# Planning the issue order of a recurrent attention kernel from a table of TensorE places, with a hand-over latency for each pair of engines

## The chip, the cores and the metric

The kernel runs on one core of one Trainium2 chip. The metric is the device time of one execution in microseconds (us), as the median over several executions. "The profile" is one execution recorded by the hardware profiler; its page and its trace give each instruction's engine, start, duration and what it waited for. In the profile PE is TensorE (PEld are its weight loads), DVE is VectorE, ACT is ScalarE, POOL is GpSimd, SP is SyncE. "L968" is a line of the kernel file; the same operation has another line number in each variant.

## The reference

Two rounds of attention with a recurrent memory and of a dense layer. All the tensors are bf16.

```python
def attention(x, mem0, Wq, Wk, Wv, Wo):        # x: 2048 x 512, 32 heads of 128
    mem = mem0                                  # 8 rows of 512
    for s in range(64):                         # 64 segments of 32 rows
        h = concat([mem, xs])                   # 40 rows
        q, k, v = h @ Wq, h @ Wk, h @ Wv
        p = softmax(mask(q k^T * scale))        # memory columns open, the rest causal
        o = (p @ v) @ Wo
        mem = o[:8]                             # read by the next segment
        outs.append(o[8:])
    return concat(outs)

x = x + attention(layernorm(x), ...);  x = x + relu(layernorm(x) @ w1) @ w2   # 512 -> 1376 -> 512
x = x + attention(layernorm(x), ...);  x = x + relu(layernorm(x) @ w1) @ w2
```

The segments of one attention are a chain: the queries of a segment need the last output projection of the segment before.

## The kernel before

Both attentions run interleaved, the second one four segments behind the first, in 68 steps. One step projects queries and keys for 5 units of heads (u0 to u4), makes scores and a softmax for each, transposes the probabilities P into PT, attends, and ends with the output projection, whose memory rows VectorE copies into HT for the next queries. Work of the values, the layernorms and the dense layers is put between.

The program is not written in issue order. Each operation is recorded in a `Plan` with its cost, what it reads and what it writes; a list scheduler in Python then chooses, when the kernel is built, the order, the buffers, and for some operations one of two engines. The framework adds the semaphores afterwards, from the memory that each instruction really touches. Two things about that matter in this case: it takes the instructions in the order in which the plan emits them, and it keeps accesses of two engines to one PSUM bank apart, even where both only read. The plan knows nothing of the second.

```python
LAT = (0.26, 0.16, 0.16, 0.20, 1.70)            # hand-over latency, one for each engine
def t_act(n): return 0.09 + 0.833e-3 * n
def t_dve(n, rate=1): return 0.085 + 1.042e-3 * n / rate
...
# order(): 3 passes, each forward (list scheduling) and backward (latest start = next priority),
# corrected by AHEAD[kind]; the best of the three is kept and emitted in order of planned start
```

One PSUM bank (`wo`, tile "st" in the profile) holds the result of the output projection, and two copies read it: VectorE takes the memory rows into HT, and ScalarE or VectorE takes the output rows into OX.

```python
plan.op(DVE, 0.15, ev, r=[wo], w=[("HTm", i)])                        # the HT copy
...
copy_op(NC4 * SEG * len(aa), rows, r=[wo, "zero ox"], w=[ox])          # the OX copy, on ACT or DVE
```

PT is copied out of PSUM in two halves, partitions 0 to 63 and 64 to 127, and each half goes to the engine that the plan finds free first.

```python
for b in range(2):
    def keep(eng, b=b):
        R = slice(64 * b, 64 * b + 64)
        copy_on(eng, PT[R, a_lo:a_hi, 0:2 * nx, b, :], tp[R, A]...)     # cut
    copy_op(n, keep, r=[tp, "zero PT"], w=[PT, (PT, b)] if b == 0 else [(PT, b)])
```

Eight loads bring the attention's weights. The plan gives each a fixed time of arrival by its place in this list.

```python
for i, part in enumerate(("v0", "v2", "q0", "k0", "q2", "k2", "o0", "o2")):
    ...
    plan.op(POOL, 1.0, dma, w=[("W", c, pc), ("W", c, pc + 1), ...], lag=0.0)
    for n in range(2):
        plan.available(("W", c, pc + n), 4.0 + LOAD * (i + 1) + ...)
```

Of the kernel before, what the change touches and what calls it, by code (L numbers as in the profile page):

```python
# [20 lines left out]



PE, ACT, DVE, POOL, SP = range(5)
LAT = (0.26, 0.16, 0.16, 0.20, 1.70)

WHOLE, COL64, EITHER = range(3)
TURN = 0.11
PASSES = 3

RULE = (0.052, 0.937, 39.167, 24.322)
AHEAD = {
    "attend.ev": -1.96, "attend.mm": -0.95, "dense_layer.mm": -0.85, "dense_layer.relu": 5.2, "finish_pair.add": -5.1,
    "finish_pair.add0": 0.5, "finish_pair.add1": -6.36, "finish_pair.turn": 2.26, "finish_pair.widen": 0.01,
    "late_values.cp": -9.2, "late_values.put": 0.92, "layernorm.aggr": -7.15, "layernorm.keep": 0.04,
    "layernorm.norm": -2.92, "layernorm.power": -0.26, "layernorm.stats": 2.48, "layernorm.turn": -30.25,
    "load_dense.dma1": -1.13, "load_dense.dma2": -2.4, "load_group.get": -0.77, "load_weights.dma": -0.55,
    "make_ident": 4.63, "make_mask": 7, "place_values.dma": 17.27, "prep_x.cp": -1.81, "prepare.get_memory": -2.96,
    "prepare.get_x": -8.86, "prepare.keep": -0.84, "prepare.place": 0.28, "prepare.zero": -0.64,
    "prepare.zero_banks": -5.82, "prepare.zero_columns": -5.11, "prepare_group.load": -0.14,  # L40
    "prepare_group.put": -0.18, "project.ev": 10.38, "project.first": 0.18, "project.mm": -0.98,
    "project.rows": -4.33, "queries_keys.ev": 4.81, "queries_keys.mm": 0.09, "scores.block": 0.96,
    "scores.exp": -1.91, "scores.keep": -25.3, "scores.mm": 0.21, "scores.mul": -8.63, "scores.recip": -1.72,
    "scores.sub": -9.57, "scores.top": 1.48, "scores.total": 48.55, "scores.turn": 1.1, "values.mm*": -36.32,
# [6 lines left out]

def t_act(n):
    return 0.09 + 0.833e-3 * n


def t_dve(n, rate=1):
    return 0.085 + 1.042e-3 * n / rate


def t_pool(n):  # L60
    return 0.06 + 2.2e-3 * n


class Pool:
# [5 lines left out]
    def reset(self):  # L70
        self.free, self.taken = [(0.0, i, None) for i in range(len(self.tiles))], 0
# [7 lines left out]
    def when(self, bufs):  # L79
        if len(self.free) < len(bufs) or self.ordered and bufs[0].no != self.taken:  # L80
            return 1e9
        return sorted(f[:2] for f in self.free)[len(bufs) - 1][0]

    def take(self, b):
        f = min(self.free, key=lambda f: f[:2])
        self.free.remove(f)
        self.taken += 1
        b.i = f[1]
        return f[2]
# [12 lines left out]
class Op:  # L102
    __slots__ = ("eng", "cost", "fn", "preds", "succs", "bufs", "new", "given", "ready", "start", "end", "wait",
                 "after", "seq", "tile", "lag", "mode", "more", "both", "spare")


class Plan:
    def __init__(self):
        self.ops, self.writer, self.readers = [], {}, {}
        self.given = {}  # L110
# [4 lines left out]
    def op(self, eng, cost, fn, r=(), w=(), tile=WHOLE, lag=None, more=0.0, spare=False):  # L115
        o = Op()
        o.both = dict(zip(eng, cost)) if isinstance(eng, tuple) else None
        if o.both:
            eng, cost = eng[0], cost[0]
        o.eng, o.cost, o.fn, o.succs, o.seq, o.tile = eng, cost, fn, [], len(self.ops), tile  # L120
        o.mode, o.more, o.spare = tile, more, spare
        o.lag = LAT[eng] if lag is None else lag
# [26 lines left out]
    def forward(self, prio):  # L149






        look, stay, far, room = RULE
        for pool in self.pools:
            pool.reset()
        for b in self.bufs:
            b.left, b.end = len(b.users), 0.0  # L160
        for o in self.ops:
            o.wait, o.ready, o.after = len(o.preds), o.given, []
        free = [0.0] * 5
        cand = [[] for _ in range(5)]
        for o in self.ops:
            if not o.wait:
                for e in o.both or (o.eng,):
                    cand[e].append(o)
        count, tile = 0, WHOLE
        while count < len(self.ops):  # L170
            best = None
            for e in range(5):
                lo, starts = None, []
                for o in cand[e]:
                    t = max(o.ready, free[e])
                    if o.both and any(max(o.ready, free[i]) + c < t + o.both[e] for i, c in o.both.items() if i != e):
                        continue
                    for pool, bufs in o.new:
                        t = max(t, pool.when(bufs))
                    starts.append((t, o))  # L180
                    if lo is None or t < lo:
                        lo = t
                if lo is not None and lo < 1e9 and (best is None or lo < best[0]):
                    best = (lo, e, starts)
            assert best is not None, "no operation can be planned"
            lo, e, starts = best
            def rank(c):
                return (prio[c[1].seq] - (stay if e == PE and c[1].tile in (tile, EITHER) else 0.0), c[1].seq)

            t, o = min((c for c in starts if c[0] <= lo + look), key=rank)  # L190
            if e == PE and o.spare:

                soon = [c for c in starts if t < c[0] < t + o.cost and prio[c[1].seq] < prio[o.seq] - far]
                if soon:
                    due = min(c[0] for c in soon)
                    t, o = min((c for c in starts if c[0] + room * c[1].cost * c[1].spare <= due and c[0] <= due), key=rank)
            o.start = t
            for i in o.both or ():
                if i != e:
                    cand[i].remove(o)  # L200
            if o.both:
                o.eng, o.cost, o.lag = e, o.both[e], LAT[e]
            cand[e].remove(o)
            for pool, bufs in o.new:
                for b in bufs:
                    last = pool.take(b)
                    if last is not None:
                        o.after += last.users
            o.end = o.start + o.cost
            if e == PE:  # L210
                o.mode = tile if o.tile == EITHER else o.tile
                if o.mode != tile:
                    o.end, tile = o.end + TURN, o.tile
                if o.mode == COL64:
                    o.end += o.more
            free[e] = o.end
            seen = o.end + o.lag
            for b in o.bufs:
                b.left -= 1
                b.end = max(b.end, seen)  # L220
                if not b.left:
                    b.pool.free.append((b.end, b.i, b))
            for s in o.succs:
                s.ready = max(s.ready, seen)
                s.wait -= 1
                if not s.wait:
                    for i in s.both or (s.eng,):
                        cand[i].append(s)
            count += 1
        return max(o.end for o in self.ops)  # L230

    def backward(self, total):

        due = [total] * len(self.ops)
        users = [list(o.preds) + o.after for o in self.ops]
        wait = [len(o.succs) for o in self.ops]
        for o in self.ops:
            for p in o.after:
                wait[p.seq] += 1
        free = [total] * 5  # L240
        heaps = [[] for _ in range(5)]
        later = [[] for _ in range(5)]

        def offer(o):
            heappush(later[o.eng], (-due[o.seq], o.seq))

        for o in self.ops:
            if not wait[o.seq]:
                offer(o)
        late, count, tile = [0.0] * len(self.ops), 0, WHOLE  # L250
        while count < len(self.ops):
            best = None
            for e in range(5):
                hi = free[e] if heaps[e] else -1e9
                if later[e]:
                    hi = max(hi, min(free[e], -later[e][0][0]))
                if best is None or hi > best[0]:
                    best = (hi, e)
            hi, e = best
            while later[e] and -later[e][0][0] >= hi - 0.05:  # L260
                o = self.ops[heappop(later[e])[1]]
                heappush(heaps[e], (-o.end, o.seq))
# [822 lines left out]
```

## Time and profile before

The median is 1677.74 us (3 runs, 1676.78 to 1678.85). The table shows where TensorE's time goes. It is worked out from the starts of all matmuls in the trace: the floor is the count of each form times its usual start-to-start spacing, and what is above it is sorted by where it occurs. (The parts overlap a little: as rounded they exceed the span by 2 us here.)

| part of the profiled 1679.0 us | us |
|---|---|
| floor: matmuls at their usual spacing | 1535 |
| 495 changes between 128- and 64-column mode, median 0.097 each | 48 |
| waits between operations | 71 |
| stalls inside operations | 27 |

These are the busy times and the shares of the chain that ended last, from the page of the kernel before.

```profile
PE 1628.4 (97%) x40568; PEld 1395.6 (83%) x40568; DVE 1066.3 (64%) x3090; ACT 1061.1 (63%) x2679; POOL 246.3 (15%) x603
...
PE 79%; DVE 13%; DMA 4%; issue 1%; POOL 1%; ACT 1%; SPq 0%; POOLq 0%; DVEq 0%; ACTq 0%
```

TensorE bounds the kernel. The next fence has lines of the view of waits of the same kernel, four of TensorE's, without those between them: engine and line, what it was idle for, total us, how often, the longest.

```profile
PEld L832 <- DVE HT L990: 9.4, 21, 0.5
PE work L832 <- DVE HT L990: 6.7, 21, 0.3
PE work L947 <- ACT PT L724: 6.1, 24, 0.3
PEld L519 <- DVE P L909: 5.4, 26, 0.9
```

The first two are the queries behind the HT copy, then attend behind PT, then the transposition of P behind the softmax. No single wait is large. By the matmul starts, waits and stalls together come to 1.84 us per two steps in steady state (steps 26 to 61).

The last view of before is that of the HT copy: its instructions, what ended the idle time of its engine, and who waited for it.

```profile
L990 DVE CAST HT<-st x67: 191/225/227, 60.3 to 1647.5; 128x64 bf16<-128x64 f32 x60, 128x32 bf16<-128x32 f32 x7
its engine sat idle before it (us, times) until:
  PE st L974: 81.3, 65
  ACT OX L724: 0.5, 1
who waited for it (us, times):
  ACT OX L724: 44.9, 65
```

The HT copy waits for TensorE, as it should, and the OX copy on ScalarE waits for the HT copy, because both read one bank and the HT copy was emitted first.

### The profile page before, as it was taken

To read this page: it belongs to the slowest core of one execution; us is meant where nothing else is said; L and a number is where in the kernel's file an instruction comes from. 1 tells how busy PE (TensorE), PEld (TensorE's weight loads), DVE (VectorE), ACT (ScalarE), POOL (GpSimd) and SP (SyncE) were. 2 spreads that over 40 slices of the span, in tenths; PEclk is the share of its full clock that TensorE was granted. 3 is DMA by queue.
4 is the path that set the end of the run, shared out by engine and by line. 5 is a ranking of instruction groups with operands and counts; after the bars stand their busy time and mean duration, and the time that the engine had idled before them with its cause. 6 is when DMAs were issued, how large, how long until landed. Compare 5 with 4: busy or idle time off the path is not lost.

```text
span 1679.0 us, 90465 instructions
## 1 busy us (share of the span) xinstructions
PE 1628.4 (97%) x40568; PEld 1395.6 (83%) x40568; DVE 1066.3 (64%) x3090; ACT 1061.1 (63%) x2679; POOL 246.3 (15%) x603
## 2 busy tenths in 40 slices
PE   6899999999999999999999999999999999999998
PEld 3578888888888888888888888888888888888886
DVE  5457576666676575667666666676566666766665
ACT  3466666666666666666666666666666666666664
POOL 3111111111111111111111111111111111111100
PEclk9999999999999999999999999999999999999999
DMA  9611111111110101000000000101010000000000
GB/s 366 239 51 35 37 39 27 35 39 34 33 39 18 37 18 31 22 21 24 19 24 21 22 20 17 27 18 26 17 27 16 21 22 21 18 20 17 18 5 7
DMA packets 32502, 64.88 MB, mean 39 GB/s; under 512 B 7048, under 2 KB 16912, under 8 KB 32112
## 3 DMA queue, kind: packets, MB, share of 16 engines
q1 hardware_dynamic: 25984, 39.38, 8.5%
q0 software_dynamic: 4608, 18.19, 2.9%
q8 instruction: 318, 5.21, 1.3%
q10 hardware_dynamic: 1520, 1.52, 0.3%
q14 instruction: 72, 0.59, 0.1%
HBM read 33.89 MB, written 12.45 MB: 28 GB/s over the span
## 4 chain that ended last, share of the span: by engine, by line
PE 79%; DVE 13%; DMA 4%; issue 1%; POOL 1%; ACT 1%; SPq 0%; POOLq 0%; DVEq 0%; ACTq 0%
PE work L832 33%; PE fill L780 16%; PE st L974 13%; PE fill L519 8%; PE work L947 3%; PE work L861 3%; DMA Wo_sb<-in_A_Wo_dram 3%; PE work L519 2%; DVE sm L886 2%; DVE OT L726 2%; DVE PT L726 2%; DVE ln L528 1%; DMA V<-vw 1%; POOL P L909 1%; DVE xg L616 1%
## 5 line engine op out<-in xcount | busy, mean ns | idle before, releaser
L832 PE MATMUL work<-HT,Wq_sb 128*128 128x80 bf16 (+1 forms) x8704 | 391.0, 200 | 8.7 <-DVE HT L990 6.7
L832 PE MATMUL work<-HT,Wk_sb 128*128 128x80 bf16 (+1 forms) x8704 | 389.7, 199 | 5.3 <-DMA Wk_sb<-in_A_Wk_dram 2.8
L974 PE MATMUL st<-OT,Wo_sb 128*128 128x80 bf16 (+1 forms) x8704 | 353.6, 200 | 3.7 <-DMA Wo_sb<-in_A_Wo_dram 3.5
L832 PEld LDWEIGHTS <-Wq_sb 128*128 128x128 bf16 x8704 | 333.0, 99 | 28.3 <-issue 9.9
L974 PEld LDWEIGHTS <-Wo_sb 128*128 128x128 bf16 x8704 | 321.7, 100 | 24.2 <-issue 17.8
L832 PEld LDWEIGHTS <-Wk_sb 128*128 128x128 bf16 x8704 | 335.9, 99 | 7.0 <-DMA Wk_sb<-in_A_Wk_dram 3.7
L872 DVE TENSOR_TENSOR es<-work,maskb 128x320 f32<-128x320 f32 (+2 forms) x340 | 137.3, 404 | 303.6 <-PE work L861 295.3
L909 POOL TENSOR_TENSOR P<-es,sm 128x160 bf16<-128x160 f32 (+1 forms) x274 | 127.5, 466 | 1212.2 <-ACT kT L724 494.2
L780 PE MATMUL fill<-Wv_sb,HT 128*64 128x512 bf16 x2176 | 282.7, 384 | 0.6 <-DVE vg L726 0.6
L724 ACT CAST qT<-work 128x320 bf16<-128x320 f32 (+1 forms) x500 | 204.6, 409 | 83.7 <-PE work L832 63.3
L724 ACT CAST kT<-work 128x320 bf16<-128x320 f32 (+1 forms) x489 | 200.0, 409 | 74.4 <-PE work L832 29.4
L724 ACT CAST PT<-work 64x320 bf16<-64x320 f32 (+2 forms) x451 | 162.7, 363 | 111.8 <-PE work L519 69.1
L724 ACT CAST vw<-fill 128x512 bf16<-128x512 f32 x221 | 129.3, 585 | 103.1 <-PE fill L780 94.6
L724 ACT CAST OT<-work 128x320 bf16<-128x320 f32 (+1 forms) x374 | 145.1, 409 | 58.7 <-PE work L947 56.9
L780 PEld LDWEIGHTS <-HT 128*64 128x64 bf16 x2176 | 102.3, 110 | 63.7 <-issue 3.2
L883 ACT ACTIVATE es<-es 128x320 f32<-128x320 f32 (+2 forms) x340 | 135.1, 404 | 23.4 <-DVE es L879 13.9
L886 DVE TENSOR_REDUCE sm<-es 128x8 f32<-128x320 f32 (+2 forms) x340 | 133.4, 399 | 25.3 <-ACT es L883 22.7
L876 DVE TENSOR_REDUCE mx<-es 128x8 f32<-128x320 f32 (+2 forms) x340 | 135.0, 397 | 3.2
L879 DVE TENSOR_TENSOR es<-es,mx 128x320 f32<-128x320 f32 (+2 forms) x340 | 134.2, 401 | 1.6
L861 PEld LDWEIGHTS <-qT 128*40 128x40 bf16 x4096 | 91.5, 98 | 43.3
L726 DVE CAST PT<-work 64x160 bf16<-64x160 f32 (+2 forms) x229 | 87.3, 381 | 60.3 <-ACT PT L724 47.0
L947 PE MATMUL work<-PT,V 128*64 128x80 bf16 (+1 forms) x1504 | 114.8, 203 | 7.5 <-ACT PT L724 5.9
(89 smaller groups left out, 1856.2 us busy)
## 6 DMA issues: line engine op xcount, KB each, us to landing
V<-vw SPq DMA_DIRECT2D x252, 48.0 KB
V<-vh SPq DMA_DIRECT2D x126, 64.0 KB
vh<-vg SPq DMA_DIRECT2D x12, 512.0 KB
Wv_sb<-in_A_Wv_dram POOLq DMA_DIRECT2D x2, 2048.0 KB, 11.1
Wq_sb<-in_A_Wq_dram POOLq DMA_DIRECT2D x2, 2048.0 KB, 22.3
Wk_sb<-in_A_Wk_dram POOLq DMA_DIRECT2D x2, 2048.0 KB, 29.2
Wo_sb<-in_A_Wo_dram POOLq DMA_DIRECT2D x2, 2048.0 KB, 42.5
vh<-w_sb SPq DMA_DIRECT2D x4, 512.0 KB
```

The costliest lines, as they stand in the source:

```text
L519: nc.tensor.matmul(out_[u:v, :], lhsT=lhsT[:, u:v], rhs=rhs, start=start, stop=stop, tile_position=(0, u))
L724: nc.scalar.copy(out=out_, in_=in_)
L726: nc.vector.tensor_copy(out=out_, in_=in_)
L780: nc.tensor.matmul(vp[64 * b:64 * b + 64, :], lhsT=cols[:, c4, :], rhs=Wv_sb[:, c4, n * 512:(n + 1) * 512], start=(c4 == 0), stop=(c4 == N ...
L832: nc.tensor.matmul(qp[:, hi * 2 * L:hi * 2 * L + n], lhsT=W_sb[:, c4, h * Dh:(h + 1) * Dh], rhs=HT[:, c4, c0:c1], start=(c4 == 0), stop=(c ...
L861: nc.tensor.matmul(v[64 * g2:64 * g2 + L, a, b, i, :], lhsT=qT[:, hi, a * L:(a + 1) * L], rhs=kT[:, hi, a * L:(a + 1) * L], start=True, st ...
L872: nc.vector.tensor_tensor(out=flat(es[:, A]), in0=flat(sp[:, A]), op=ALU.add, in1=maskb[:, a_lo:a_hi, :].unsqueeze(2).to_broadcast([128, n ...
L883: nc.scalar.activation(out=es[:, A], in_=es[:, A], func=ACTF.Exp, scale=SCALE)
L886: nc.vector.tensor_reduce(out=sm[:, As], in_=es3(), axis=AX.X, op=ALU.add)
L909: (nc.gpsimd if eng == POOL else nc.vector).tensor_tensor(out=o, in0=e, in1=sv.unsqueeze(3).to_broadcast([128, na, 2, L]), op=ALU.mult)
L947: nc.tensor.matmul(o[u:u + cols, :, a, :], lhsT=V[:, p, e0 + u:e0 + u + cols], rhs=PT[:, a, 2 * i + h2, :, :], start=True, stop=True, tile ...
L974: nc.tensor.matmul(wo[:, 2 * W * c4 + c0:2 * W * c4 + c1], lhsT=Wo_sb[:, h, c4 * 128:(c4 + 1) * 128], rhs=OT[:, h, c0:c1], start=(h == 0 a ...
```

## The change

The change replaces the planner and its model, and nothing of what is computed: both kernels record the same 9896 operations with the same dependencies. The three passes become one. TensorE's operations get their priority from a table, by their place in a period of two steps; the operations of the other engines get theirs from their successors. The latencies become a table with one entry for each pair of engines, and the costs are made smaller. The table looks as if it was searched for by trial.

```diff
-LAT = (0.26, 0.16, 0.16, 0.20, 1.70)
+LAT = ((0.0, 0.20, 0.21, 0.26, 0.26), (0.155, 0.14, 0.14, 0.20, 0.20), (0.145, 0.18, 0.125, 0.23, 0.23),
+       (0.13, 0.13, 0.10, 0.10, 0.20), (1.7, 1.7, 1.7, 1.7, 1.7))     # rows: from, columns: to; PE ACT DVE POOL SP
-TURN = 0.11
-PASSES = 3
+TURN = 0.096
+PERIOD = 17.9985
+PLACE = {
+    ("attend.mmu0.0", 0): 181.486, ("attend.mmu0.0", 1): 97.524, ...    # cut: one number per operation and step parity
+}
 def t_act(n):
-    return 0.09 + 0.833e-3 * n
+    return 0.05 + 0.833e-3 * n
 def t_dve(n, rate=1):
-    return 0.085 + 1.042e-3 * n / rate
+    return 0.065 + 1.042e-3 * n / rate
+    def rank_ops(self):
+        for o in reversed(self.ops):
+            if PE in o.cost:
+                o.prio = PERIOD * o.step + PLACE.get((o.key, o.step % 2), 0.0)
+            else:
+                e, c = min(o.cost.items(), key=lambda x: x[1])
+                o.prio = min((s.prio - (LAT[e][min(s.cost)] if o.lag is None else o.lag) for s in o.succs),
+                             default=PERIOD * (o.step + 3)) - c - AHEAD.get(o.kind, 0.0)
-    def forward(self, prio): ...      # cut
-    def backward(self, total): ...    # cut
```

A few costs of single operations change by some hundredths, those of GpSimd's copies by more (0.06 + 0.0013 n in place of 0.06 + 0.0022 n for n columns), and AHEAD and the scheduler's four thresholds (RULE) get new numbers. The intent is to fill TensorE's waits.

## The prediction

> **What bounds it now.** TensorE, in issue order. The page gives it busy 1628.4 of 1679.0 us (97%); the granted clock is 1.00 from 200 to 1600 us (stretches view). Busy includes pipeline fill, so I worked from start-to-start spacings in the matmul timeline: 35.8 ns per 128x80 matmul, 25 per 128x40, 217 per pair of 128x512 on two column halves. Over all 40568 matmuls that makes 1535 us of streaming (an estimate). The other 143 us, by sums over the same starts:
>
> - 495 changes between 128- and 64-column matmuls, median 97 ns extra: 48 us. The Trainium skill, "TensorEngine Tiling (Array Packing)", Performance Considerations, says a change of tiling mode drains TensorE; this trace agrees.
> - waits between operations, 71 us. Some 20 lie in the first 60 us (weights landing, first layernorms). From 200 to 1600 us they are about 1.35 us per two steps (48 us): queries behind HT after the last output projection, 0.49 us in even steps from 24 on; attend of the last unit behind PT copies, 0.42; turns of P behind the softmax chain, 0.2 and 0.12; a layernorm turn, 0.13.
> - 28 us inside operations, then tail.
>
> **What the change does.** Arithmetic and dependencies stay; order, engine choice and buffer rotation change. From the two built orders:
>
> - Mode changes fall from 495 to 445: -5 us, all critical. 256 matmuls fewer, as 64-column pairs became single ones; a pair already takes the time of a single, so worth nothing.
> - VectorE takes 144 more P multiplies from GpSimd (352 against 482 ns in the group list) and half of the PT copies; ScalarE nearly all value and query/key copies. By the listed means each gains 10 to 30 us of busy time; at 64% and 63% neither bounds.
> - Slack, in TensorE work between producer and consumer, in steady steps: last unit's attend 1.29 us, was 1.15, and its PT halves now go to two engines, so the 0.42 us wait should mostly go. Softmax to turn 5.0, was 4.6: the 0.2 us wait goes. Values to attend through the V transfer 5.15, was 4.97. Layernorm turn behind the dense layer 4.83, was 4.25.
> - Against it: in even steps the queries still follow the last projection at once, now from step 14 on, and HT's input rows have only 0.57 us from their layernorm turn. That chain (copy 0.37, GpSimd copy 0.29, hand-overs of about 0.2) needs about 1.1 us. So 0.5 us stays in some 26 steps: 13 to 14 us, was 10.
> - Start: DMA order unchanged; 1 us more TensorE work is placed before the last Wo part. Tail: about the same.
>
> **Sum.** Mode changes -5; steady waits -8 to -14; ramp -1; collisions on VectorE +2. About -16 us, 1%.
>
> **Predicted time 1662 us, 8 in 10 between 1648 and 1677.** Faster by over 2% 0.12, within 2% 0.86, slower by over 2% 0.02.
>
> **What would show it.** Right: 445 mode changes; TensorE busy share towards 98%; waits behind PT copies and P nearly gone, about 0.5 us before queries in even steps left, on HT's copies; GpSimd busy down by about 65 us. Wrong: waits of TensorE behind VectorE grow (the plan packed the softmax chain too tightly); matmul spacings or the granted clock change (my floor is wrong).
>
> **What would make it wrong.** Chains are judged one at a time: VectorE queueing can lengthen one with slack on paper, above all the single-head unit with 3.0 us (was 3.7). Or the table fits so well that nearly all steady waits go (then about 1645).

## The result, and the profile after

The kernel after takes 1729.76 us (4 runs, 1727.27 to 1731.04) against 1677.83 for the kernel before in the same rounds (4 runs). The ratio is 1.031, with a 95% interval of 1.029 to 1.032: 3.1% slower. The granted clock is 0.992 against 0.995.

These are the same two lines of the page, for the kernel after.

```profile
PE 1643.3 (95%) x40309; PEld 1400.7 (81%) x40312; DVE 1091.3 (63%) x3205; ACT 1061.3 (61%) x2708; POOL 188.3 (11%) x459
...
PE 61%; DVE 26%; ACT 5%; issue 4%; DMA 3%; POOL 2%; SPq 0%; ACTq 0%; DVEq 0%; POOLq 0%
```

TensorE's share falls from 97 to 95%. The chain that ended last runs through VectorE for 26% of the span where it was 13%. The waits of TensorE in the kernel after, in the view of waits (lines between them are left out):

```profile
PEld L810 <- DVE HT L968: 23.0, 29, 0.9
PE work L810 <- DVE HT L968: 18.6, 26, 0.7
PEld L497 <- DVE P L887: 16.9, 65, 0.9
PE st L952 <- DVE OT L704: 12.7, 29, 0.4
PE fill L758 <- DMA Wv_sb<-in_A_Wv_dram: 10.8, 1, 10.8
```

The waits for HT and for P have grown 2.4- to 3.1-fold (PEld 9.4 to 23.0 us, PE 6.7 to 18.6, P 5.4 to 16.9). Two are new: the first output projection of a step (L952) waits for a copy of the attended rows (OT) on VectorE, and one early group of values waits 10.8 us for a weight. That of attend behind ScalarE's PT, 6.1 us before, is gone from the list.

The sums over the matmul starts say where the 52 us came from (50 us in the two profiled spans; the rounded parts add up to 55). The last column shows what the prediction had.

| part, us | before | after | change | predicted |
|---|---|---|---|---|
| mode changes (495, now 445) | 48 | 43 | −5 | −5 |
| waits between operations | 71 | 104 | +33 | −9 to −15 |
| stalls inside operations | 27 | 54 | +27 | not named |
| waits and stalls in steady state, per two steps | 1.84 | 3.07 | +1.23 | −0.2 to −0.4 |
| end of step 0's last projection, at us | 60.1 | 73.0 | +13 | 1 us of work added |

The lateness against the kernel before is 12.9 us at the end of step 0, 24.3 at step 24, 49.0 at step 64 and 52.0 at step 67, the last (what follows it is 2 us shorter). So a quarter comes at the start, and the rest grows step by step. From step 24 to 64 it grows by 1.24 us per two steps, which agrees with the 1.23 in the table.

Three differences stand out when all engines are compared, not TensorE alone.

**The loads.** These are GpSimd's first loads in the timeline of the kernel before; the columns are start, duration, engine, line, operation.

```profile
1.34 1.71 POOL L394 DMA_DIRECT2D Wv_sb<-in_A_Wv_dram  x2 [0.83 <-POOLq L1066]
...
7.01 0.79 POOL L394 DMA_DIRECT2D Wq_sb<-in_A_Wq_dram  x1
7.80 0.74 POOL L394 DMA_DIRECT2D Wk_sb<-in_A_Wk_dram  x1
```

And of the kernel after:

```profile
2.36 0.97 POOL L372 DMA_DIRECT2D Wv_sb<-in_A_Wv_dram  x1
3.33 0.76 POOL L372 DMA_DIRECT2D Wq_sb<-in_A_Wq_dram  x1
4.07 0.76 POOL L372 DMA_DIRECT2D Wk_sb<-in_A_Wk_dram  x1
4.79 1.19 POOL L369 DMA_DIRECT2D Wo_sb<-in_A_Wo_dram  x1
5.95 0.78 POOL L372 DMA_DIRECT2D Wv_sb<-in_A_Wv_dram  x1
```

Before, both halves of Wv, which TensorE needs first, were issued first. Now the second half is issued fifth, behind three loads for later. TensorE pays for it, as its own timeline of the kernel after shows (the bracket gives the idle time before the group, and what ended it):

```profile
33.88 3.62 PE L758 MATMUL fill<-Wv_sb,XG 128*64 128x512 bf16 x16 [10.79 <-DMA Wv_sb<-in_A_Wv_dram]
...
53.51 0.72 PE L810 MATMUL work<-HT,Wq_sb 128*128 128x40 bf16 x16 [3.38 <-DMA Wq_sb<-in_A_Wq_dram]
```

**The two copies out of one bank.** The view of the HT copy, now for the kernel after:

```profile
L968 DVE CAST HT<-st x67: 191/224/226, 73.5 to 1698.4; 128x64 bf16<-128x64 f32 x60, 128x32 bf16<-128x32 f32 x7
its engine sat idle before it (us, times) until:
  ACT OX L702: 119.0, 67
```

All 67 HT copies now wait for the OX copy, which was the other way round before. The timelines show one such place each, first before, then after.

```profile
1040.59 0.23 DVE L990 CAST HT<-st 128x64 bf16<-128x64 f32 x1 [1.55 <-PE st L974]
1040.85 0.37 ACT L724 CAST OX<-st 128x256 bf16<-128x256 f32 x1 [0.24 <-DVE HT L990]
```

```profile
853.06 0.37 ACT L702 CAST OX<-st 128x256 bf16<-128x256 f32 x1 [0.20 <-PE st L952]
853.46 0.23 DVE L968 CAST HT<-st 128x64 bf16<-128x64 f32 x1 [1.36 <-ACT OX L702]
```

The HT copy starts 0.40 us later, when the OX copy has ended, and the queries of the next step wait for it: 0.89 us instead of 0.49 in the even steps, 0.21 instead of 0 in the odd ones.

**The halves of PT.** In both kernels a PT half may go to either engine, but the plan now mostly gives the upper half to VectorE: 224 times (187 with the lower one on ScalarE, 37 with both), where it was 122 times. In the trace, VectorE takes longer over it. Three instructions back to back in step 31 of the kernel after; the middle one writes partitions 64 to 127:

```profile
840.08 0.49 DVE L854 TENSOR_REDUCE mx<-es 128x8 f32<-128x320 f32 x1
840.60 0.49 DVE L704 CAST PT<-work 64x320 bf16<-64x320 f32 x1
841.12 0.49 DVE L857 TENSOR_TENSOR es<-es,mx 128x320 f32<-128x320 f32 x1
```

From start to start it takes 0.52 us, twice. The recorded duration is 0.49 us, so each one started only when the one before had ended. Over the trace of the kernel before, the spacing from a 64x320 copy to the next instruction without idle time is 0.408 us for a lower half (37 cases) and 0.525 for an upper half (48 cases); for 64x160 it is 0.242 and 0.359. So an upper half costs VectorE about 0.12 us before it and 0.12 us after it. ScalarE shows the same step after its own PT copies in this trace: 0.322 us for a lower 64x320 half (61 cases) and 0.445 for an upper one (75 cases), though the recorded durations are equal (0.42 us). The Trainium skill, "VectorE: DVE Perf Modes", section "Two Vector instructions with no wait between them", gives a model that fits: a Vector instruction is held until every earlier one has finished if its input or output starts in another group of 32 partitions than in the last instruction that read, or wrote, the same memory (SBUF or PSUM). A copy that starts at partition 64 among others that start at 0 is held, and the next one too. The section speaks of VectorE alone. The new cost model says 0.065 + 0.00104 × 320 = 0.398 us, which fits the lower half and is 0.127 us short for the upper.

### The profile page after: what moved, and what is told of

It reads as the page before. It is cut to its first block, busy times and chain, and to the rows that moved or that the text cites. A ratio compares the mean times of both kernels' runs of the same rounds, so it can differ in the third digit from the quotient of the medians. Undisturbed runs are those within 1.5% of the kernel's fastest.

```text
span 1729.2 us, 89659 instructions
## 1 busy us (share of the span) xinstructions
PE 1643.3 (95%) x40309; PEld 1400.7 (81%) x40312; DVE 1091.3 (63%) x3205; ACT 1061.3 (61%) x2708; POOL 188.3 (11%) x459
## 4 chain that ended last, share of the span: by engine, by line
PE 61%; DVE 26%; ACT 5%; issue 4%; DMA 3%; POOL 2%; SPq 0%; ACTq 0%; DVEq 0%; POOLq 0%
PE work L810 31%; PE fill L758 11%; PE st L952 9%; PE fill L497 5%; DVE PT L704 5%; DVE sm L864 3%; DVE P L887 3%; DVE mx L854 3%; DVE es L857 3%; DMA Wq_sb<-in_A_Wq_dram 3%; PE work L839 3%; DVE es L850 2%; PE work L925 2%; PE work L497 1%; DVE sm L867 1%
## 5 line engine op out<-in xcount | busy, mean ns | idle before, releaser
L810 PE MATMUL work<-HT,Wq_sb 128*128 128x80 bf16 (+1 forms) x8704 | 373.3, 199 | 23.5 <-DVE HT L968 18.6
L810 PE MATMUL work<-HT,Wk_sb 128*128 128x80 bf16 (+1 forms) x8704 | 369.7, 200 | 0.0
L952 PE MATMUL st<-OT,Wo_sb 128*128 128x80 bf16 (+1 forms) x8704 | 347.3, 199 | 12.7 <-DVE OT L704 12.7
L952 PEld LDWEIGHTS <-Wo_sb 128*128 128x128 bf16 x8704 | 318.8, 99 | 31.2 <-issue 29.1
L810 PEld LDWEIGHTS <-Wk_sb 128*128 128x128 bf16 x8704 | 326.0, 100 | 18.2 <-issue 15.2
L702 ACT CAST qT<-work 128x320 bf16<-128x320 f32 (+1 forms) x539 | 216.8, 409 | 91.2 <-PE work L810 59.4
L702 ACT CAST kT<-work 128x320 bf16<-128x320 f32 (+1 forms) x506 | 207.5, 410 | 65.9 <-PE work L810 30.6
L702 ACT CAST vw<-fill 128x512 bf16<-128x512 f32 x271 | 158.1, 583 | 103.6 <-PE fill L758 99.9
L702 ACT CAST PT<-work 64x320 bf16<-64x320 f32 (+1 forms) x340 | 119.9, 353 | 134.3 <-PE work L497 77.5
L704 DVE CAST PT<-work 64x320 bf16<-64x320 f32 (+2 forms) x340 | 138.4, 407 | 29.5 <-ACT PT L702 10.6
L887 POOL TENSOR_TENSOR P<-es,sm 128x160 bf16<-128x160 f32 (+1 forms) x130 | 60.0, 461 | 813.6 <-DVE sm L867 577.6
L887 DVE TENSOR_TENSOR P<-es,sm 128x160 bf16<-128x160 f32 (+1 forms) x414 | 137.1, 359 | 3.4
```

Source lines behind the costliest of these rows:

```text
L702: nc.scalar.copy(out=out_, in_=in_)
L704: nc.vector.tensor_copy(out=out_, in_=in_)
L810: nc.tensor.matmul(qp[:, hi * 2 * L:hi * 2 * L + n], lhsT=W_sb[:, c4, h * Dh:(h + 1) * Dh], rhs=HT[:, c4, c0:c1], start=(c4 == 0), stop=(c ...
L887: (nc.gpsimd if eng == POOL else nc.vector).tensor_tensor(out=o, in0=e, in1=sv.unsqueeze(3).to_broadcast([128, na, 2, L]), op=ALU.mult)
L952: nc.tensor.matmul(wo[:, 2 * W * c4 + c0:2 * W * c4 + c1], lhsT=Wo_sb[:, h, c4 * 128:(c4 + 1) * 128], rhs=OT[:, h, c0:c1], start=(h == 0 a ...
```

## The experiments

The theory has three parts: the loads, the order of the two copies, the upper halves. The rivals were that the packed plan, with its smaller latencies and costs, is too tight as a whole, and, for the halves, that VectorE simply has too much work. All the kernels gave correct results. The differences in the text are those of medians against the kernel after, which was run in its own rounds; the kernel before, which ran beside each of them, had medians of 1677.8 to 1678.7 on all four occasions. All the edits of the kernel after but those of e8 and e12 work on the finished plan (e9 changes the model too), between sorting and emission:

```diff
-        return sorted(self.ops, key=lambda o: (o.start, o.seq))
+        plan = sorted(self.ops, key=lambda o: (o.start, o.seq))
+        ...                                     # the edit
+        return plan
```

### e1_loads: the kernel after, with the eight loads in the order of their list

```diff
+        loads = [o for o in plan if o.kind == "load_weights.dma"]
+        for o, fn in zip(loads, [o.fn for o in sorted(loads, key=lambda o: o.seq)]):
+            o.fn = fn
```

> The changed kernel, with the eight weight loads issued in the order of the kernel before (v0 v2 q0 k0 q2 k2 o0 o2) in the same eight slots of GpSimd's queue; nothing else moves. Theory (the start is late because the changed plan issues the second half of Wv, Wk and Wq last): the end of step 0, 12.9 us late, comes back by 8 to 12 us (ident and mask still come in the changed order), so about 1719 us. Rival (the start is late because of the later identity matrix, layernorms and first turns, not of the weights): under 4 us.

Measured: 1720.0 us, ratio to before 1.025 (1.0234 to 1.0265). That is 9.8 us less than after. Step 0's last projection ended at 62.3 us instead of 73.0, and TensorE no longer waited for Wv or Wq, only 4.8 us for Wo; the steady waits stayed at 3.06 us. The loads cost 10 us, once.

### e2_ht_first: the kernel after, with the HT copy emitted ahead of the OX copy

```diff
+        for ev in [o for o in plan if o.kind == "project.ev"]:
+            at = [i for i, o in enumerate(plan) if o.kind == "project.rows" and o.step == ev.step]
+            if at and at[0] < plan.index(ev):
+                plan.remove(ev); plan.insert(at[0], ev)
```

No engine's own order changes by this; the two copies are on different engines. Only which one of them waits for the other changes.

> The changed kernel, with the copy of the memory rows into HT put ahead of the copy into OX of the same step; no engine's own order changes, only which of the two waits for the other. Theory (both read one PSUM bank, the second is held until the first is done, and the change put HT second): the wait of the queries drops from 0.89 to about 0.5 us in even steps and from 0.21 to 0 in odd ones, 33 times 0.6 is 20 us, so about 1710 us. Rival (the whole plan is too tight because its latencies and costs are too small, and another chain takes over at once): under 6 us.

Measured: 1714.39 us, ratio 1.0215 (1.0200 to 1.0231): 15.4 us less than after. The view of the HT copy in this variant:

```profile
its engine sat idle before it (us, times) until:
  PE st L958: 92.9, 66
```

The queries' wait went back from 0.889 to 0.485 us in even steps and from 0.212 to 0 in odd ones, and the other steady waits did not move.

### e3_both: e1 and e2 together

> Both edits together. If they are separate losses, the gains add up: about 31 us, 1698 us, still some 20 us slower than the kernel before, which is left for the steady waits on VectorE. If they share a cause, clearly less than the sum.

Measured: 1704.54 us, ratio 1.0155 (1.0138 to 1.0172). It is 25.2 us less than after, the sum of 9.8 and 15.4. About 26 us of the difference to before was left, and its waits were those for P, and for the OT copy in the first projection.

### e4_before_ox_first: the kernel before, with the OX copy emitted ahead of the HT copy

```diff
+        for rows in [o for o in plan if kind[o.seq] == "project.rows"]:
+            at = [i for i, o in enumerate(plan) if kind[o.seq] == "project.ev" and set(o.preds) & set(rows.preds)]
+            if at and at[0] < plan.index(rows):
+                plan.remove(rows); plan.insert(at[0], rows)
```

> The kernel before, with the copy into OX put ahead of the copy into HT, as in the changed one; no engine's own order changes. Theory: the hand-over from the last projection to the queries goes from 0.49 to 0.89 us; cover is 0 in 22 even steps (+0.4 us each) and 0.67 us in 33 odd ones (+0.2 us each): about +16 us, 1694 us. Rival: no change within 3 us.

Measured: 1694.32 us, ratio 1.0094 (1.0079 to 1.0109): this order alone makes the kernel before 16 us slower. Its queries waited 0.89 and 0.21 us, as in the kernel after. Here the new planner has no part in it.

### e12_tie: the kernel after, with one number of its table changed

```diff
-LAT = ((0.0, 0.20, 0.21, 0.26, 0.26), ...
+LAT = ((0.0, 0.21, 0.21, 0.26, 0.26), ...
```

Why did the order flip? The table says that a result of TensorE reaches ScalarE in 0.20 us and VectorE in 0.21. So the plan starts the OX copy 0.01 us ahead of the HT copy, and emits it first. With a tie, the recorded order decides, and that has the HT copy first.

> The changed kernel with one number changed: the latency from TensorE to ScalarE in the table 0.21 instead of 0.20, equal to that to VectorE. In the built order 66 of 67 copies into HT then wait for TensorE alone (0 of 67 in the changed kernel). Theory: it gains what e2_ht_first gained, 15 us, so about 1714, give or take 10 for the rest of the plan that this number also moves. If the plan is as brittle as the two re-planned kernels showed (1849 us), it may be far worse.

Measured: 1713.79 us, ratio 1.0215 (1.0199 to 1.0230), the same as e2. Its view of the HT copy:

```profile
  PE st L952: 92.6, 66
  ACT OX L702: 0.2, 1
```

So the flip came from 10 nanoseconds in the plan, and was worth 16 us on the chip. The plan was made anew here, but little else moved: when both kernels are built, TensorE's order differs in 2 operations, ScalarE's in 7 and VectorE's in 8.

### e5_lower_half: e3, and VectorE takes the lower half of PT where it had the upper one

```diff
+        for up in [o for o in plan if o.kind == "scores.keep" and o.eng == DVE]:
+            low = [o for o in plan if o.seq == up.seq - 1]
+            if low[0].kind == "scores.keep" and low[0].eng == ACT:
+                up.fn, low[0].fn = low[0].fn, up.fn
```

In 187 places the two engines exchange their halves. Each engine has as many instructions as before, of the same size and in the same slots. If VectorE just had too much work, this would change nothing.

> The kernel of e3_both (changed kernel with the loads in the old order and HT's copy first; 1704.5 us), with the two PT copies of a unit exchanged wherever VectorE had the upper 64 partitions and ScalarE the lower: VectorE now copies the lower ones. Which engine waits for the other is unchanged. Theory A (a VectorE copy that starts at partition 64 between instructions that start at 0 is held until the one before is finished, and holds the next: in the trace of the changed kernel 0.12 us each, about 10 copies per two steps): VectorE gets back up to 2 us per two steps, the 0.6 us wait inside the first projection, and the layernorm waits, shrink: 10 to 25 us less. Theory B (what makes VectorE late is waiting for ScalarE's half in the same PSUM bank): under 4 us.

Measured: 1678.99 us, ratio 1.0006 (0.9989 to 1.0022): 25.6 us less than e3, and the time of the kernel before. The same place in its timeline (the middle instruction now writes partitions 0 to 63):

```profile
812.86 0.49 DVE L867 TENSOR_REDUCE mx<-es 128x8 f32<-128x320 f32 x1
813.26 0.47 DVE L717 CAST PT<-work 64x320 bf16<-64x320 f32 x1
813.66 0.48 DVE L870 TENSOR_TENSOR es<-es,mx 128x320 f32<-128x320 f32 x1
```

The spacing is 0.40 us, twice, where it was 0.52. Two lines of the view of waits of this variant:

```profile
PEld L510 <- DVE P L900: 10.4, 38, 0.9
...
PE work L823 <- DVE HT L981: 8.2, 26, 0.3
```

The wait for HT is near what it was before (8.2 us, then 6.7), that for P fell from 16.9 to 10.4, and the wait of the first projection for VectorE's OT copy is no longer listed (it was 12.7). By the starts, that projection's stall went from 0.61 to 0.135 us per two steps. ScalarE now pays for the upper half. These are its copy of the other half at the same place and the instruction behind it, first in the kernel after (a lower half), then in e5 (an upper half):

```profile
841.13 0.42 ACT L702 CAST PT<-work 64x320 bf16<-64x320 f32 x1 [0.81 <-DVE PT L704]
841.45 0.58 ACT L702 CAST vw<-fill 128x512 bf16<-128x512 f32 x1
```

```profile
813.76 0.42 ACT L715 CAST PT<-work 64x320 bf16<-64x320 f32 x1 [0.67 <-DVE PT L717]
814.21 0.58 ACT L715 CAST vw<-fill 128x512 bf16<-128x512 f32 x1
```

The duration is the same, but the spacing goes from 0.32 to 0.45 us. So the exchange does not remove the holds, it moves them: VectorE's busy time falls from 1091.2 us (e3) to 1070.1, and ScalarE's rises from 1062.6 to 1077.1. On VectorE they made TensorE wait; on ScalarE most of them do not.

### e10_swap_only: the kernel after, with the exchange of e5 and nothing else

> The changed kernel with the exchange of PT halves alone (loads and HT's copy stay as changed). If the three losses are separate, it gains what it gained on top of e3_both, 25 us: 1704 us.

Measured: 1703.28 us, ratio 1.0153 (1.0139 to 1.0167): 26.5 us less than after, as in the presence of the other two. Stalls inside operations fell from 53.7 to 29.9 us. So the three causes add: 9.8 + 15.4 + 26.5 = 51.7, and the difference to explain was 51.9.

### e6_halves_act: e3, with every PT half on ScalarE

```diff
+        for up in [o for o in plan if o.kind == "scores.keep" and o.eng == DVE]:
+            up.eng = ACT
```

> e3_both with both PT copies of every unit on ScalarE, at the places where they stood in the order. No wait between the two engines for a bank is left, no copy from partition 64 on VectorE; ScalarE gets about 10 copies of 0.33 us more per two steps. Theories A and B both say VectorE catches up (wait inside the first projection 0.6 to 0, layernorm turns 0.47 to under 0.15, turns of P less): 15 to 30 us less than 1704.5, unless ScalarE becomes late in turn. Rival C (VectorE is late because of the four multiplies moved to it from GpSimd, not because of the copies): under 6 us.

Measured: 1682.34 us, ratio 1.0029 (1.0015 to 1.0044), 22.2 us less than e3. VectorE's holds are gone and its busy time falls to 961.6 us; ScalarE's rises to 1180.4, and the scores of unit u3 wait 0.52 us for it in odd steps, where they did not wait. This edit takes away the holds and the work at once, so alone it can't tell them apart. Beside e5 it can: taking over 100 us of work off VectorE helps no more than exchanging the halves and leaving it there. So VectorE's load need not be cut to win the time back: what cost it was where the data of VectorE's copies start.

### e7_before_lower_half: the kernel before, with the same exchange

> The kernel before, with the same exchange of PT halves as in e5_lower_half wherever VectorE had the upper and ScalarE the lower one (90 of the 340 pairs; in the changed kernel it was 187). Theory A (copies from partition 64 hold VectorE, 0.12 us on either side, in every kernel): VectorE gets 90 times 0.24, about 22 us of its time, back; of the steady waits of 1.84 us per two steps those behind turns of P (0.2, 0.09) and attend (0.43) shrink: 5 to 15 us less than 1678, so 1663 to 1673 us. Rival (only the changed plan is sensitive to it): within 3 us of 1678.

Measured (5 rounds): 1673.33 us, ratio 0.9975 (0.9962 to 0.9987). The old plan has 90 such places, and the exchange gains 4.7 us there, just under the 5 to 15 that were expected: the transposition of P lost its wait (0.20 to 0 us per two steps), but the next waits took a part of it back (P of u4 from 0.09 to 0.235). This small version beats both kernels.

### e11_head: e5, with GpSimd's first instructions in the order of the kernel before

The edit in words:

```diff
+        first = the first two loads, make_ident, make_mask
+        rest = the other six loads
+        plan = first + everything up to the second layernorm power + rest + everything else
```

> e5_lower_half with GpSimd's first instructions in the kernel before's order: two Wv loads, identity, mask, two powers, then the other loads. The end of step 0 was still 2.6 us late: about 1676.5 us, 2.5 less than e5_lower_half.

Measured (5 rounds): 1677.17 us, ratio 0.9997 (0.9984 to 1.0009). The time came near the expected, but it is only 1.8 us below e5, about as much as the runs of one kernel spread, and the reason did not hold: step 0's last projection ended at 63.0 us, no earlier than in e5 (62.7). The view of waits says why: TensorE's wait for the identity matrix from GpSimd (7.7 us in e5) went, but one for the load of the memory rows (6.0 us) came in its place, and that for the first layernorms on VectorE grew from 10.9 to 16.5 us. What else keeps the start of the new plan 3 us behind stays open. Two things in its trace point to where to look: GpSimd issues the six other loads only at 13.8 us (7.0 in the kernel before), since the layernorm powers ahead of them in its queue wait for VectorE; and at 59.5 us attend waits 3.1 us for the transfer of the values, where the kernel before has no such wait in step 0.

### e8_bank_in_plan: the plan is told of the three orders, and plans anew

```diff
-            plan.op(POOL, 1.0, dma, w=[("W", c, pc), ...
+            plan.op(POOL, 1.0, dma, w=["load order", ("W", c, pc), ...
-            copy_op(n, keep, r=[tp, "zero PT"], ...
+            copy_op(n, keep, r=[tp, "zero PT", *([(PT, 0)] if b else [])], ...
-            copy_op(NC4 * SEG * len(aa), rows, r=[wo, "zero ox"], w=[ox])
+            copy_op(NC4 * SEG * len(aa), rows, r=[wo, "zero ox", ("HTm", i)], w=[ox])
```

> The changed kernel, whose planner is told three orders[...]: loads in the order of their table, OX's copy after HT's, the upper PT copy after the lower. The table of places stays. If the hidden orders are the whole of the loss, the plan made with them is as good as e3_both or better: 1680 to 1700 us. If the table of places fits only the plan it was searched with, worse than e3_both: over 1706.

Measured: 1849.75 us, ratio 1.1023 (1.1006 to 1.1039), with a granted clock of 0.958. Of the two outcomes the second came, far beyond its bound: worse than e3. What it was to mend, it did mend: the loads went out in order, and the HT copies waited for TensorE alone (66 of the 67 had a wait). But everything else became worse: 501 mode changes, waits of 200 us, stalls of 64.

The table of places seems to fit only the model it was made with: with three more dependencies it no longer fits. Which of the three breaks the plan was not tested, and e12 shows that a small change does not. The edits of the finished plan were therefore the better instrument: they leave all else in place.

### e9_old_latencies: e3, planned with the old latencies and costs

```diff
-LAT = ((0.0, 0.20, 0.21, 0.26, 0.26), ...
+LAT = tuple((x,) * 5 for x in (0.26, 0.16, 0.16, 0.20, 1.70))
-TURN = 0.096                                    # and t_act, t_dve: back to 0.09 and 0.085
+TURN = 0.11
```

> e3_both, planned with the latencies (one per engine), the ScalarE and VectorE costs and the mode-change cost of the kernel before; the table of places stays. Theory (what is left is the PT copies, which neither set of numbers knows): within 8 us of 1704.5. Rival (the new numbers are too small, so the plan is too tight): under 1692.

Measured: 1848.37 us, ratio 1.1014 (1.0998 to 1.1031), clock 0.951. It was to test whether the plan is too tight, and it can't: as in e8, it shows only that the table does not bear this other model. That question is answered by e5 instead, which keeps the packed order with all its latencies and is as fast as the kernel before. The order as a whole is not what made the kernel slow.

## Why the prediction was wrong

The prediction said 1662 us (1648 to 1677); the result was 1729.76, and the 2% chance of "slower" came true. Three terms of its sum failed: "collisions on VectorE +2" (measured 26, as holds), "steady waits -8 to -14" (the queries' wait for HT alone cost 15 more) and "ramp -1" (the loads cost 10 more).

- **"Mode changes fall from 495 to 445: -5 us"**: right. The trace has 445, worth 4.9 us. (What the prediction takes from the Trainium skill, "TensorEngine Tiling (Array Packing)", that a change of tiling mode drains TensorE, stands in its section "Tiling Modes"; the trace shows the 0.097 us, not the draining itself.)
- **"the 0.42 us wait should mostly go"** (attend of the last unit): right, 0.43 to 0.08 us. **"the 0.2 us wait goes"** (a transposition of P behind the softmax): right for the wait ahead of it, but 0.185 us came back inside the operation (0.025 before), and other units gained waits: 0.24 and 0.20 us. **"Layernorm turn ..., was 4.25"**: its wait did not go but grew, 0.13 to 0.31 us. The slacks had been read as TensorE work between producer and consumer; what grew was the time that VectorE took in between.
- **"collisions on VectorE +2"**: this is the term that was mis-sized most. It measured about 26 us (e10, and e5 against e3). The prediction counted the halves of PT that VectorE got, and its busy time did rise by 25 us as foreseen, at 63% of the span (with the exchange in both kernels, e5 against e7, it rises by 14.6, so some 10 of the 25 were more holds). But it priced a copy with the mean of its group, and did not ask which half it was, though the trace of before held both spacings, 0.408 and 0.525 us. "VectorE queueing can lengthen one with slack on paper" stood among what could make it wrong; it got no number.
- **"So 0.5 us stays in some 26 steps: 13 to 14 us, was 10"**: mis-sized. The wait before the queries measured 0.89 us in even steps, and 0.21 in odd ones where there was none. The chain was judged from HT's input rows and their layernorm. The copy that matters is the HT copy out of the bank, and the order of the two readers of that bank had not been looked at. It cost 15 us (e2, e12), and e4 shows the same 16 us in the kernel before. The Trainium skill, "PSUM — Partial Sum Buffer", section "PSUM bank collisions raise a hardware error", says that two engines on one bank must be guarded, readers too; all 67 waits in the trace after agree. (It also says that different groups of 32 partitions may be accessed at once. The framework orders by the whole bank, so no run here shows that.)
- **"Start: DMA order unchanged; 1 us more TensorE work"**: false. GpSimd issues the second half of Wv fifth instead of second, and Wo ahead of it; this cost 10 us (e1). TensorE's and the other engines' orders had been compared, that of GpSimd's queue not.
- **"ScalarE nearly all value and query/key copies ... each gains 10 to 30 us of busy time"**: VectorE gained 25, ScalarE 0.2 (1061.1 to 1061.3). GpSimd lost 58 us (about 65 was expected). As the prediction said, neither engine's share bounds.
- **The signs named in advance** worked: TensorE's share went to 95 and not to 98%, and "waits of TensorE behind VectorE grow" came true. The cause offered there, a softmax chain packed too tightly, was not it.

With the three causes taken out, the new plan is as fast as the old one and not 1% faster (e5 and e11: 1679.0 and 1677.2 us, though its steady waits are 1.65 and 1.62 us per two steps, below the 1.84 of before, and it has 50 mode changes fewer). The new plan is better only in steady state. Its start is 3 us behind, and in steps 2 to 23 its waits and stalls are 1.34 us per two steps in e5 and 1.35 in e11, where those of before are 0.92: 0.42 × 11 = 4.6 us more. Of the 50 mode changes that the new plan saves, 46 lie in just these steps and pay for this. Attend behind the transfer of the values waits 4.5 us over the whole span in e5 (1.3 before), 4.0 of them in steps 0 and 1, so at the start. No run tested what causes either.

## What to carry to other kernels

When a planner moves instructions, compare the queue of every engine, the issue order of the loads and the direction of each wait between engines before pricing anything: a tie that turns by 10 ns in the model decided 15 us here, since the framework enforces an order that the plan does not know. Price an instruction by where its data starts, by what stands beside it and by the engine that it is on, not by the mean of its group; and compare the spacing from start to start, since the recorded duration did not show the hold. And a table of places may not outlive the model it was made with (e8, e9): to test one of its parts, edit the finished order and don't plan anew.

## What the Trainium skill lacked or had wrong

- "VectorE: DVE Perf Modes", section "Two Vector instructions with no wait between them": its rule of the held instruction fits the spacings measured here, but it gives no cost. One hold took 0.12 us here (0.408 to 0.525 us from a 64x320 copy to the next instruction, 0.242 to 0.359 for 64x160), both on the copy at partition 64 and on the instruction behind it, and exchanging 187 such copies took 26 of 1730 us away. The section speaks of VectorE alone, and no page was found that says it of ScalarE; ScalarE showed the same step (0.322 to 0.445 us for 64x320, 0.188 to 0.311 for 64x160).
- "PSUM — Partial Sum Buffer", section "PSUM bank collisions raise a hardware error": it says that readers of one bank must be guarded, but not that the guard gives the readers an order which can be the wrong one for the critical path. A reader whose result nobody needed soon came ahead of the urgent one in all 67 steps and held it up (0.40 us at the place shown), worth 15 to 16 us.
- "TensorEngine Tiling (Array Packing)", section "Tiling Modes": it says that a change of tiling mode drains TensorE, and gives no size. Here it was 0.097 us in the median.
- No page was found that says what the order of issue does to weight loads at the start: a load issued three places later landed so late that TensorE stood still for 10.8 us.
